# Sliding-window attention and a spectral mix on one core: more weight buffers at the end of the attention stage, a new order of stage memory, and x moved within the forward transform

## The chip, the core and the metric

The kernel runs on one core of a Trainium2 chip. Its engines are called here as the profile calls them: PE (TensorE, matmuls; PEld are its weight loads), DVE (VectorE), ACT (ScalarE), POOL (GpSimd) and SP (SyncE). Data come from HBM over 16 DMA engines into SBUF, the memory of 128 partitions that all engines read; matmuls write to PSUM. The metric is the device time of one execution in microseconds, the median of several runs.

## What is computed

Two parts follow each other. The first is attention with a causal window of 64 positions, for 8 batches of 8 heads, 576 positions of 64 numbers. The second takes the attention's output as x (8 x 576 x 512), transforms it along the sequence, multiplies each of the lowest 64 modes by its own complex 512 x 512 matrix, transforms back, adds x, and passes the sum through one more 512 x 512 matrix.

```python
# attention, per batch and head
scores = q @ k.T / sqrt(64)
mask = (rel >= 0) & (rel < 64)           # rel = query position - key position
x = softmax(where(mask, scores, -1e9)) @ v
# spectral mix, x now [8, 576, 512]
X = rfft(x, axis=1)
Xr, Xi = X[:, :64].real, X[:, :64].imag
Yr = einsum('bmd,mde->bme', Xr, w_r) - einsum('bmd,mde->bme', Xi, w_i)
Yi = einsum('bmd,mde->bme', Xr, w_i) + einsum('bmd,mde->bme', Xi, w_r)
u = x + irfft(Yr + 1j * Yi, n=576)
out = u + maximum(u @ w_ch, 0)
```

All inputs are fp32 in HBM. The two sets of mode weights, w_r and w_i, are 64 matrices of 1 MB each, 134 MB in all. They are read once, and cast to bf16 by the DMA on the way: each of the 128 weights is 512 KB in SBUF, 4,096 bytes in every partition.

## The kernel before

The kernel has three stages, and the weights are loaded beneath the first two.

**The attention stage** goes over 36 windows of 8 blocks of 64 queries. For each batch it loads q, k and v, transposes q and k and regroups v with matmuls (ten "units" a batch, spread over the windows), adds the mask by a matmul with an identity, adds the scores, takes the exponential on ACT, and weighs v with it. The sums land in `pso` and DVE divides them into `x_sb`. When a batch is complete, `dft` makes its forward transform into `XQ`. Every load is issued by POOL, in program order.

```python
VW = 4 * 17; LW = 5; EW = 13
x_sb = keep.tile([128, B, NT, NC, 128], BF16, name="x_sb")

def load_w(i, pool, tag, wt=None):
    m, im = divmod(i, 2)
    if wt is None:
        wt = pool.tile([128, NC, DM], BF16, name="wt", tag=tag)
    src = moe_w_i if im else moe_w_r
    nc.gpsimd.dma_start(out=wt, in_=src[m].rearrange("(p c) e -> p c e", c=NC))
    wtiles[i] = wt

def mask(w, times):
    for _ in range(times):
        for hh in range(2):
            nc.tensor.matmul(out=pss[(2 * w + hh) % 3], lhsT=ident_bf,
                             rhs=view(band, 0, [[0, WIN // 128], [1, 128]]), ...)
# ... in weigh(), when a head is complete:
rcp = small.tile([128, 2, NT * 4], FP32, name="rcp")
nc.vector.reciprocal(out=rcp, in_=view(pso, 16, [[512, 2], [17, NT * 4]]))
nc.vector.tensor_tensor(
    out=view(x_sb, b * NT * DM + g * 16, [[64, 2], [128, NT * 4], [1, 16]]),
    in0=view(pso, 0, ...), in1=view(rcp, 0, ...), op=ALU.mult)

def dft(b):
    ps = ps_misc.tile([128, NC, 2, NM], FP32, name="psx", tag="misc")
    for c in range(NC):
        for t in range(NT):
            n = rows(t)
            nc.tensor.matmul(out=ps[:, c, :, :], lhsT=x_sb[:n, b, t, c, :],
                             rhs=trigF[:n, t, :], start=(t == 0), stop=(t == NT - 1))
    nc.vector.tensor_copy(out=view(XQ, ...), in_=ps...)
    nc.scalar.mul(out=view(XQ, ...), in_=ps[:, :, 1, :], mul=-1.0)
```

The heads' columns stand in `x_sb` in an order that suits the transform's weight loads, (part of a head, head, 16 columns), and not in the order of the output.

The weights' buffers in this stage: 5 in `wlate` and 13 in `wearly`, loaded two at the start and three behind each batch's units; then the buffers of q, k and v of the last two batches as those become free (`spare_raw`, three for each); then, at window 32, batch 6's kT and the two halves of its vt.

```python
def unit(b, j):
    units[b][j]()
    if j == NU - 1:                     # the last of ten units of a batch
        if b + 2 < B:
            load(b + 2)                 # q, k, v two batches ahead
        early(3)                        # weights into wlate, wearly
        if b >= B - 2:
            early(EARLY)
            spare_raw()
# ... at the end of window w:
if w == -(-9 * (B - 1) // 2):
    i = (B - 2) % 2
    spare(kTs[i])
    for j in range(2):
        spare(vts[i][:, j])
```

**The mode stage** multiplies mode by mode: 32 matmuls a mode, 16 columns each. It starts with eight more weight buffers, `wmid`, and then goes round the five `wlate` buffers. Beside the first 48 modes it transposes x and multiplies it by w_ch (`channel`, 36 tiles). For that, each tile of `x_sb` is first put into the order of the output, by a copy on ACT and one back on DVE. Beside the last 16 modes it turns the lower part of the spectrum back and adds it to the channel product (`spectrum`, `second`).

```python
late = p2.enter_context(tc.tile_pool(name="late", bufs=1, side="right", ...))
YT, YTl = ...; trigI, trigL = ...; wch = late.tile([128, NC, DM], FP32R, name="wch")
Z0a = late.tile([128, 33, DM], FP32R, name="Z0a")
MW = 8
wmid = wm.enter_context(tc.tile_pool(name="wmid", bufs=MW, side="right", ...))
while nw < MID:                          # MID = nw + MW
    load_w(nw, wmid, "wm"); nw += 1
# ... after each mode m:
while nw < 2 * NM and (nw - MID if nw < MID + LW else nw - LW) <= 2 * m + 1:
    load_w(nw, wlate, "wl"); nw += 1

def channel(i):
    ...
    xc = xtp.tile([128, NC, 128], BF16, name="xc")
    nc.scalar.copy(out=xc[:n], in_=x_sb[:n, bb, tt, :, :])                      # L493
    nc.vector.tensor_copy(out=view(x_sb[:n], (bb * NT + tt) * DM, [[NC, 128], [1, NC]]),
                          in_=view(xc[:n], 0, [[1, 128], [128, NC]]))           # L494
    ...  # transpose, copy, four matmuls by wch, copy to Z0
```

The scheduler puts these two copies early: they run in the attention stage.

**The output stage** begins when mode 63 is done: `turn` brings back the last 16 modes, `group` sums four tiles at a time, and SP writes them out. All its matmuls on `Yb`, `trigI`, `trigL`, `Z0` are of 512 columns.

Of the kernel before, what the change touches and what calls it, by code (L numbers as in the profile page):

```python
# [26 lines left out]
def kernel(  # L27
# [19 lines left out]
    VW = 4 * 17  # L47
    RUN = S // 32
    LW = 5
    EW = 13  # L50

# [20 lines left out]
    x_sb = keep.tile([128, B, NT, NC, 128], BF16, name="x_sb")  # L72
# [10 lines left out]
    etp = p1.enter_context(tc.tile_pool(name="etp", bufs=4, side="right"))  # L83
    small = p1.enter_context(tc.tile_pool(name="small", bufs=2, side="right"))
# [51 lines left out]
    def gen_trig(pool, mt, n, dst_cos, dst_sin, tag):  # L136

        f = pool.tile([128, 2, n], FP32, name="gf" + tag)
        r = pool.tile([128, 2, n], FP32, name="gr" + tag)
# [8 lines left out]
    with tc.tile_pool(name="tmpf", bufs=1, side="right") as tmp:  # L148
        mo = tmp.tile([128, NM], FP32, name="mo")
        to = tmp.tile([128, NT], FP32, name="to")  # L150
        mt = tmp.tile([128, NT * NM], FP32, name="mtf")
# [4 lines left out]
        nc.vector.tensor_tensor(out=view(mt, 0, [[NM, NT], [1, NM]]), in0=view(mo, 0, [[0, NT], [1, NM]]),  # L156
                                in1=view(to, 0, [[1, NT], [0, NM]]), op=ALU.mult)
        gen_trig(tmp, mt, NT * NM, trigF[:, :, 0:NM], trigF[:, :, NM:2 * NM], "f")
# [15 lines left out]
    band = acons.tile([128, 128], BF16, name="band")  # L174
    nc.vector.memset(band, 0.0)
    for half in range(2):
        pp = slice(64 * half, 64 * half + 64)
        own = band[pp, 64 * half:64 * half + 64]
        nxt_ = band[pp, 64 - 64 * half:128 - 64 * half]
# [9 lines left out]
    vts = [p.tile([128, 2, 4, 9, 4, 17], BF16, name=f"vt{i}") for i, p in enumerate((aeven, acons))]  # L189
    for vt in vts:  # L190
        nc.vector.memset(vt[:, 0, :, :, :, 16:17], 1.0)
# [12 lines left out]
    def transpose_units(b):  # L204
# [18 lines left out]
        def vpart(a, j0, j1):  # L223
            def f():
# [8 lines left out]
                for i in range(2):  # L233
                    evac(vt[:, 0, 2 * a + i, j0:j1, :, 0:16],
                         view(pss[i], 0, [[D, n], [1, 4], [4, 16]]), i == 0)
# [14 lines left out]

    def mask(w, times):

        for _ in range(times):
            for hh in range(2):
                nc.tensor.matmul(out=pss[(2 * w + hh) % 3], lhsT=ident_bf,  # L255
                                 rhs=view(band, 0, [[0, WIN // 128], [1, 128]]),
                                 start=True, stop=False, skip_group_check=True)
# [28 lines left out]
    def weigh(w, G0, G1):  # L286
        et = ets[w]
        for hh in range(2):
            for G in range(G0, G1):
# [7 lines left out]
                nc.tensor.matmul(out=pso[po, hh, (i // 2) * VW:(i // 2 + 1) * VW],  # L297
                                 lhsT=et[pk, hh, col:col + 64],
                                 rhs=vt[pk, 1 - f % 2, 2 * hh + g // 2, f // 2, :, :],
                                 start=True, stop=True, skip_group_check=True)  # L300
        if G1 > G0 and G1 % 9 == 0:

            rcp = small.tile([128, 2, NT * 4], FP32, name="rcp")
            nc.vector.reciprocal(out=rcp, in_=view(pso, 16, [[512, 2], [17, NT * 4]]))
            nc.vector.tensor_tensor(  # L305
                out=view(x_sb, b * NT * DM + g * 16, [[64, 2], [128, NT * 4], [1, 16]]),
                in0=view(pso, 0, [[512, 2], [17, NT * 4], [1, 16]]),
                in1=view(rcp, 0, [[NT * 4, 2], [1, NT * 4], [0, 16]]), op=ALU.mult)
            if g == 3:
                dfts.append(b)  # L310

    def dft(b):
        ps = ps_misc.tile([128, NC, 2, NM], FP32, name="psx", tag="misc")
        for c in range(NC):
            for t in range(NT):
                n = rows(t)
                nc.tensor.matmul(out=ps[:, c, :, :], lhsT=x_sb[:n, b, t, c, :],  # L317
                                 rhs=trigF[:n, t, :], start=(t == 0), stop=(t == NT - 1))
# [5 lines left out]
    EARLY = LW + EW  # L324

    def early(n):
        nonlocal nw
        for _ in range(n):
            if nw < EARLY:
                load_w(nw, wlate if nw < LW else wearly, "wl" if nw < LW else "we")  # L330
# [422 lines left out]
```

The softmax here doesn't subtract the row's maximum and nothing guards it: scores larger than these inputs give would overflow.

## Time and profile before

| | |
|---|---|
| time, median of 3 runs | 450.59 us (449.89 to 457.41) |
| span of the profiled execution | 449.9 us |
| PE busy | 343.5 us (76%) |
| DVE busy | 209.4 us (47%) |
| ACT busy | 156.1 us (35%) |
| POOL busy | 131.5 us (29%) |
| moved by DMA | 92.49 MB, 206 GB/s in the mean |
| read from HBM, written to it | 163.58 MB, 9.44 MB |

How to read it: busy shares are averages over three stages that have different limits, so a stage has to be looked at by itself. The strip of 40 slices shows how full each engine is as time goes on, 11.25 us to a slice; PEclk in it is the matmul clock that was granted, in tenths; GB/s counts the bytes as they are written, and a weight is written at half the size at which it is read. The attention stage ends at about 148 us, the last weight lands at 405.4 us, and what follows is the output stage. A group's line gives how many instructions, their busy time and the mean of one, and then how long the engine was idle before them and for what.

### The profile page before, as it was taken

How to read it: one execution, taken by the hardware profiler on the slowest of the kernel's cores; microseconds unless marked ns; L12 is line 12 of the kernel's file. 1: busy time of each engine (PE TensorE's matmuls, PEld its weight loads, DVE VectorE, ACT ScalarE, POOL GpSimd, SP SyncE). 2: the span in 40 equal slices, each digit the busy share in tenths (PEclk: the TensorE clock that was granted, in tenths of full speed). 3: DMA queues.
4: the chain of work that ended last, by engine and by line, in shares of the span. 5: the costliest groups of instructions: out<-in, count | busy, mean ns of one | idle time of the engine just before them, and what ended most of it. 6: DMA issues, size and time to landing. Idle time of an engine off the chain costs nothing.

```text
span 449.9 us, 11402 instructions
## 1 busy us (share of the span) xinstructions
PE 343.5 (76%) x4996; PEld 223.8 (50%) x4996; DVE 209.4 (47%) x412; ACT 156.1 (35%) x295; POOL 131.5 (29%) x218
## 2 busy tenths in 40 slices
PE   6899999999999765588887874322275775898994
PEld 2366556556655665465565653212253443555552
DVE  4466897888876400145545421000024433344774
ACT  4566776767865300041233221000010100103563
POOL 8632532442120411122222221121122122112574
PEclk9989999999999555595889998555555657698999
DMA  8999999999997799999999999999999999990787
GB/s 139 206 209 208 212 210 208 212 208 208 214 169 146 136 213 213 258 205 213 203 214 213 214 212 215 214 212 214 213 214 213 213 210 212 215 194 23 245 298 276
DMA packets 38338, 92.49 MB, mean 206 GB/s; under 512 B 3472, under 2 KB 12688, under 8 KB 38288
## 3 DMA queue, kind: packets, MB, share of 16 engines
q0 software_dynamic: 33040, 82.32, 94.9%
q1 hardware_dynamic: 5248, 9.44, 5.9%
q8 instruction: 39, 0.64, 0.5%
q14 instruction: 11, 0.09, 0.1%
HBM read 163.58 MB, written 9.44 MB: 385 GB/s over the span
## 4 chain that ended last, share of the span: by engine, by line
DMA 37%; PE 26%; issue 17%; DVE 8%; POOL 5%; ACT 5%; POOLq 1%; ACTq 0%; DVEq 0%
DMA wt<-in_moe_w_r_dram 26%; DMA wt<-in_moe_w_i_dram 9%; PE pso L297 4%; DVE x_sb L494 3%; POOL wt L119 3%; PE psx L317 3%; PE psc L680 2%; PE psu L698 2%; DMA rv<-in_v_dram 2%; PE pst L216 2%; PE pss_186 L255 2%; ACT et L279 1%; PE pss_184 L255 1%; ACT xc L493 1%; PE pss_185 L255 1%
## 5 line engine op out<-in xcount | busy, mean ns | idle before, releaser
L465 PE MATMUL psy<-XQ,wt 128*128 128x16 bf16 x960 | 58.8, 191 | 51.3 <-DMA wt<-in_moe_w_i_dram 51.1
L119 POOL DMA_DIRECT2D wt<-in_moe_w_i_dram x60 | 33.2, 553 | 180.3 <-PE psy L465 147.1
L460 PE MATMUL psy<-XQ,wt 128*128 128x16 bf16 x944 | 60.6, 191 | 32.0 <-DMA wt<-in_moe_w_r_dram 25.4
L465 PEld LDWEIGHTS <-wt 128*128 128x128 bf16 x960 | 45.7, 104 | 63.0 <-DMA wt<-in_moe_w_i_dram 61.6
L460 PEld LDWEIGHTS <-wt 128*128 128x128 bf16 x944 | 45.6, 104 | 47.7 <-DMA wt<-in_moe_w_r_dram 37.0
L503 PE MATMUL psz<-wch,xT 128*128 128x512 f32 x144 | 49.9, 481 | 1.7 <-DMA wch<-in_moe_w_ch_dram 1.7
L500 DVE CAST xT<-pxt 128x512 fp32r<-128x512 bf16 x36 | 24.2, 687 | 53.3 <-PE pxt L497 37.5
L505 ACT CAST Z0a<-psz 128x512 fp32r<-128x512 f32 x33 | 19.4, 586 | 66.4 <-PE psz L503 51.9
L59 DVE CAST YT<-psy 128x256 fp32r<-128x256 f32 x6 | 2.5, 424 | 75.8 <-PE psy L465 75.8
L119 POOL DMA_DIRECT2D wt<-in_moe_w_r_dram x59 | 32.0, 543 | 17.0 <-PE psy L465 6.2
L620 DVE TENSOR_TENSOR Z0a<-pse,Z0a 128x512 fp32r<-128x512 f32 x33 | 21.8, 688 | 31.5 <-PE pse L597 31.5
L503 PEld LDWEIGHTS psz<-wch,xT 128*128 128x128 f32 x144 | 30.1, 230 | 6.9 <-DMA wch<-in_moe_w_ch_dram 1.8
L708 POOL TENSOR_TENSOR ot<-ot,r 128x512 f32<-128x512 f32 x18 | 22.8, 1283 | 24.7 <-ACT Yb L58 19.5
L297 PEld LDWEIGHTS <-et 128*64 128x64 bf16 (+1 forms) x576 | 22.3, 108 | 15.0 <-issue 8.0
L493 ACT COPY xc<-x_sb 128x512 bf16<-128x512 bf16 (+1 forms) x40 | 23.9, 619 | 15.1 <-DVE x_sb L494 8.8
L58 ACT CAST YT<-psy 128x256 fp32r<-128x256 f32 x6 | 2.2, 373 | 71.7 <-DVE YT L59 59.0
L494 DVE COPY x_sb<-xc 128x512 bf16<-128x512 bf16 (+1 forms) x40 | 23.1, 598 | 8.2 <-PE psx L317 3.8
L305 DVE TENSOR_TENSOR x_sb<-pso,rcp 128x640 bf16<-128x640 f32 x32 | 26.4, 824 | 1.1
L103 POOL DMA_DIRECT2D rv<-in_v_dram x32 | 20.7, 653 | 9.7 <-PE psv_348 L231 3.6
L701 ACT ACTIVATE r<-psc 128x512 f32<-128x512 f32 x36 | 19.0, 601 | 10.2 <-PE psc L686 9.6
L597 PE MATMUL pse<-yw,trigI 96*128 96x512 f32 x40 | 20.6, 584 | 0.0
L614 ACT CAST yw<-psw 96x512 fp32r<-96x512 f32 x8 | 4.7, 583 | 44.8 <-PE psw L610 44.8
(298 smaller groups left out, 668.1 us busy)
## 6 DMA issues: line engine op xcount, KB each, us to landing
wt<-in_moe_w_i_dram POOLq DMA_DIRECT2D x60, 512.0 KB, 8.6
wt<-in_moe_w_r_dram POOLq DMA_DIRECT2D x59, 512.0 KB, 10.6
out_dram<-ot SPq DMA_DIRECT2D x32, 256.0 KB, 2.4
rk<-in_k_dram POOLq DMA_DIRECT2D x8, 576.0 KB, 11.1
rq<-in_q_dram POOLq DMA_DIRECT2D x8, 576.0 KB, 10.5
rv<-in_v_dram POOLq DMA_DIRECT2D x32, 144.0 KB, 10.0
wch<-in_moe_w_ch_dram POOLq DMA_DIRECT2D x1, 1024.0 KB, 15.7
out_dram<-ot SPq DMA_DIRECT2D x8, 128.0 KB, 2.5
```

Source lines behind the costliest of these rows:

```text
L103: nc.gpsimd.dma_start(out=rv[32 * hp:32 * hp + 32, :, :, :].rearrange("r j c d -> r j (c d)"), in_=vf[hp].rearrange("(j r c) d -> r j (c d ...
L119: nc.gpsimd.dma_start(out=wt, in_=src[m].rearrange("(p c) e -> p c e", c=NC))
L297: nc.tensor.matmul(out=pso[po, hh, (i // 2) * VW:(i // 2 + 1) * VW], lhsT=et[pk, hh, col:col + 64], rhs=vt[pk, 1 - f % 2, 2 * hh + g // 2, ...
L305: nc.vector.tensor_tensor(out=view(x_sb, b * NT * DM + g * 16, [[64, 2], [128, NT * 4], [1, 16]]), in0=view(pso, 0, [[512, 2], [17, NT * 4 ...
L460: nc.tensor.matmul(out=psy[:, m % MG, e, :], lhsT=wr[:, c, ee], rhs=XQ[:, c, :, 1:3, m], start=(c == 0), stop=False)
L465: nc.tensor.matmul(out=psy[:, m % MG, e, :], lhsT=wi[:, c, ee], rhs=XQ[:, c, :, 0:2, m], start=False, stop=(c == NC - 1))
L493: nc.scalar.copy(out=xc[:n], in_=x_sb[:n, bb, tt, :, :])
L494: nc.vector.tensor_copy(out=view(x_sb[:n], (bb * NT + tt) * DM, [[NC, 128], [1, NC]]), in_=view(xc[:n], 0, [[1, 128], [128, NC]]))
L500: nc.vector.tensor_copy(out=xT, in_=pst)
L503: nc.tensor.matmul(out=psz, lhsT=xT[:, c, :], rhs=wch[:, c, :], start=(c == 0), stop=(c == NC - 1))
L620: nc.vector.tensor_tensor(out=channel_out(i), in0=ps, in1=channel_out(i), op=ALU.add)
L708: nc.gpsimd.tensor_tensor(out=ot, in0=ot, in1=r, op=ALU.add)
```

## The change

The change works on four things.

- **Room for weights in the attention stage.** One more early buffer (`wextra`), and more of the last two batches' own buffers: at window 32 batch 6's kT and vt as before and a qT, at windows 35 and 36 batch 7's kT, a qT and its vt. The early loads are spread thinner, two behind a batch instead of three.
- **Stage memory.** `late` holds only YT, YTl and wch. The seven `wmid` buffers come right behind it, so that they lie on the early buffers 6 to 12, and each is loaded as soon as the mode that used that buffer is done (`free_at`). The tables and Z0 (now one tile) come last, over the attention's memory. `Yb` and `yw` use the wmid buffers afterwards.
- **x in the forward transform.** DVE writes `x_sb` in the order of the output right away, so that the two copies of L493 and L494 are gone. The transform takes the table as its stationary side and 512 columns of x at once, five matmuls in place of 20; the result is copied by ACT and turned by four transposes one window later (`dft_turn`).
- **Smaller things.** From window 6 the mask is added in four 64 x 64 pieces; batch 1's units have another order; the tables are made in smaller pieces; four idle matmuls follow mode 63; there are 11 output buffers instead of 9.

```diff
-    VW = 4 * 17
+    VW = 66
+    XW = 1
-    x_sb = keep.tile([128, B, NT, NC, 128], BF16, name="x_sb")
+    x_sb = keep.tile([128, B, NT, DM], BF16, name="x_sb")
@@ band: two halves -> two patterns for each half of the partitions
-    band = acons.tile([128, 128], BF16, name="band")
-    for half in range(2):
+    band = acons.tile([128, 2, 128], BF16, name="band")
+    for i in range(4):                    # two affine_selects each
@@ mask
+                if w < 6:
+                    ...                   # as before, from band2
+                    continue
+                for half in range(2):
+                    pp = slice(64 * hh, 64 * hh + 64)
+                    nc.tensor.matmul(out=pss[(2 * w + hh) % 3][64 * half:64 * half + 64, :],
+                                     lhsT=ident_bf[pp, pp],
+                                     rhs=view(band[pp], 128 * half, [[0, WIN // 128], [1, 128]]),
+                                     start=True, stop=False, skip_group_check=True)
@@ weigh
-            rcp = small.tile([128, 2, NT * 4], FP32, name="rcp")
+            rcp = small.tile([128, 2, NT], FP32, name="rcp")
-                out=view(x_sb, b * NT * DM + g * 16, [[64, 2], [128, NT * 4], [1, 16]]),
+                out=view(x_sb, b * NT * DM + g * D, [[4 * D, 2], [DM, NT], [1, D]]),
@@ dft
-        for c in range(NC):
-            for t in range(NT):
-                nc.tensor.matmul(out=ps[:, c, :, :], lhsT=x_sb[:n, b, t, c, :],
-                                 rhs=trigF[:n, t, :], start=(t == 0), stop=(t == NT - 1))
+        for t in range(NT):
+            n = rows(t)
+            nc.tensor.matmul(out=ps, lhsT=trigF[:n, t, :], rhs=x_sb[:n, b, t, :],
+                             start=(t == 0), stop=(t == NT - 1))
+        Xs[b] = xsp.tile([128, NC, 128], BF16, name="Xs")
+        evac(Xs[b], view(ps, 0, [[1, NC], [NC, 128]]), True)
+    def dft_turn(b):
+        ps = ps_misc.tile([128, NC, 2, NM], BF16, name="pxq", tag="misc")
+        for c in range(NC):
+            nc.tensor.transpose(out=ps[:, c, :, :]..., in_=Xs[b][:, c, :], identity=ident_bf)
@@ early weights
-    EARLY = LW + EW
+    EARLY = LW + EW + XW
-        early(2)                          # at the start
+        early(1)
+            order = (1, 2, 4, 5, 7, 8, 0, 3, 6, 9) if b == 1 else range(NU)
-                early(3)                  # behind a batch
+                early(2)
@@ spares
-            if w == -(-9 * (B - 1) // 2):
-                i = (B - 2) % 2
+            if w in (NWIN - 4, NWIN - 1):
+                i = (B - 2) % 2 if w == NWIN - 4 else (B - 1) % 2
                 spare(kTs[i])
+                spare(qtp.tile([128, 4, S], BF16, name="qT"))
+            if w in (NWIN - 4, NWIN):
+                i = (B - 2) % 2 if w == NWIN - 4 else (B - 1) % 2
                 for j in range(2):
                     spare(vts[i][:, j])
@@ memory and weights of the mode stage
-    trigI = late.tile(...); trigL = late.tile(...); Z0a = late.tile([128, ZA, DM], ...)
+    MW = 7
+    wmid = p2.enter_context(tc.tile_pool(name="wmid", bufs=MW, side="right", ...))
+    late2 = ...                           # trigI, trigL, Z0
-    while nw < MID:
-        load_w(nw, wmid, "wm")
+    N0 = nw
+    free_at = [(LW + 6 + j) // 2 for j in range(MW)]
+        while nw < 2 * NM:                # after each mode m
+            j = nw - N0
+            if j < LW:
+                at, pool, tag = j // 2, wlate, "wl"
+            elif j < LW + MW:
+                at, pool, tag = free_at[j - LW], wmid, "wm"
+            elif j < 2 * LW + MW:
+                at, pool, tag = (nw - LW - MW) // 2, wlate, "wl"
+            else:
+                at, pool, tag = (nw - LW) // 2, wlate, "wl"
+            if m < at:
+                break
+            load_w(nw, pool, tag)
@@ channel
-                nc.scalar.copy(out=xc[:n], in_=x_sb[:n, bb, tt, :, :])
-                nc.vector.tensor_copy(out=view(x_sb[:n], ...), in_=view(xc[:n], ...))
-        Z_M = 15
+        Z_M = 17
@@ end
+                    idle(4)               # behind mode 63
-        op = p3.enter_context(tc.tile_pool(name="op", bufs=9, ...))
+        op = p3.enter_context(tc.tile_pool(name="op", bufs=11, ...))
```

## The prediction, made before the change was run

> **What bounds the kernel now.** I read four views, in this order: the page's strip of 40 slices with the queue and chain parts, to find the resource that stays full; the busy time by stretches around the one place where it isn't; the GpSimd engine's order of time there, to see who holds the transfers back; and the chain of waits through two batches of the attention stage, to see what that stage is made of.
>
> From the page (a slice is 11.25 us):
>
> ```profile
> PE   6899999999999765588887874322275775898994
> PEclk9989999999999555595889998555555657698999
> DMA  8999999999997799999999999999999999990787
> GB/s 139 206 209 208 212 210 208 212 208 208 214 169 146 136 213 213 258 205 213 203 214 213 214 212 215 214 212 214 213 214 213 213 210 212 215 194 23 245 298 276
> q0 software_dynamic: 33040, 82.32, 94.9%
> DMA 37%; PE 26%; issue 17%; DVE 8%; POOL 5%; ACT 5%; POOLq 1%; ACTq 0%; DVEq 0%
> ```
>
> The transfers are the only thing full from start to 405 us. The matmul clock sits at half speed over much of the mode stage, which is itself a sign of a PE that waits. Three weak spots: the first slice, slices 12 to 14 (169, 146 and 136 GB/s), and the output stage after the last weight. The 82.32 MB of queue 0 at the 213 GB/s of the full slices is 386 us; the loads end at 405.4. So about 19 us less some start-up is what a perfect schedule could still win.
>
> By stretches of 5 us (engine, busy us and count; then clock, DMA share, GB/s):
>
> ```profile
> 120.00:125.00 5.00, 4.80 (x84) 2.74 (x82) 4.81 (x10) 4.66 (x10) 0.53 (x1) 1.00 1.06 204
> 125.00:130.00 5.00, 4.65 (x81) 2.71 (x79) 4.56 (x9) 3.56 (x8) 1.06 (x2) 1.00 0.88 155
> 130.00:135.00 5.00, 4.75 (x77) 2.55 (x78) 2.79 (x6) 2.17 (x4) 1.42 (x3) 1.00 1.03 179
> 135.00:140.00 5.00, 5.00 (x66) 2.88 (x64) 2.85 (x6) 3.00 (x6) 0.16 (x1) 1.00 1.06 213
> 140.00:145.00 5.00, 4.36 (x82) 2.68 (x81) 3.32 (x7) 2.90 (x6) 0.00 (x0) 1.00 0.57 116
> 145.00:150.00 5.00, 3.83 (x45) 2.56 (x44) 2.79 (x5) 1.14 (x2) 1.55 (x3) 0.77 0.08 7
> 150.00:155.00 5.00, 4.05 (x104) 3.57 (x104) 3.97 (x7) 2.75 (x5) 3.43 (x7) 0.50 1.01 193
> ```
>
> Against 213 the shortfalls are 9 + 58 + 34 + 0 + 97 + 206 + 20 = 424 GB/s, times 5 us = 2.12 MB, which is **9.95 us of transfer** at 213.
>
> GpSimd, which issues every load, in order of time there:
>
> ```profile
> 134.10 0.53 POOL L119 DMA_DIRECT2D vt_178<-in_moe_w_r_dram  x1 [2.56 <-PE pso L297]
> 134.62 0.54 POOL L119 DMA_DIRECT2D vt_178<-in_moe_w_i_dram  x1
> 148.45 0.53 POOL L119 DMA_DIRECT2D wt<-in_moe_w_i_dram  x1 [13.29 <-DVE x_sb L305]
> ```
>
> After the ninth spare buffer there is nowhere to put weight 27: the next place lies over attention memory and waits 13.29 us for the last x write. That is the hole.
>
> The chain of waits from 73 to 105.1 us, two batches, by line:
>
> ```profile
> by line: PE pso L297 12.8%; DVE x_sb L494 12.0%; PE psx L317 10.7%; PE pst L216 6.0%; PE pss_186 L255 5.2%; ACT xc L493 5.2%; ACT et L279 4.9%; PE pss_184 L255 4.7%; DVE XQ L320 3.7%; PE pss_185 L255 3.4%; DVE qT L59 2.7%; DVE x_sb L305 2.6
> ```
>
> No DMA is in it: the attention stage runs at the pace of its engines. One batch takes 16.05 us (the transforms' first matmuls stand at 40.86, 72.96 and 105.06 us). Its transfers are rk 576 + rq 576 + rv 4 x 144 KB and three weights of 512 KB, 3,264 KB = 3.34 MB, or 16.0 us at 209 GB/s. So compute and transfers are matched there, and that must be watched when either changes.
>
> **What the Trainium skill says.** *Perfetto Trace Analysis*, section "Roofline": one core alone is bounded by its 16 DMA engines at about 435 GB/s. The queue writes bf16 and reads fp32, so 213.5 GB/s written is 427 read: the trace agrees, and no change of buffers will make a full slice fuller. *DMA: Bandwidth & Descriptors*, "Anatomy of one DMA — SWDGE (gpsimd) path": DMA engines don't wait on semaphores; the issuing sequencer does, before dispatch. The 13.29 us above, with 7 GB/s at the end of it, is that. *TensorEngine Tiling (Array Packing)*, "Key Properties": tiles of the array work independently, and a change of tiling mode drains it. The trace agrees on the first: 18 score matmuls on 64x64 tiles, of 64 to 128 columns, pass in 0.35 us (85.97 to 86.32 in the chain), where one 512-column mask takes 0.22. It shows no drain by itself. *TensorE: Matmul & The Clock Gate*, "Part 1: The HAM clock gate": an idle window of some 3.4 us halves the clock; the 0.50 from 150 to 180 us, with PE waiting for weights, agrees.
>
> **The change, part by part.**
>
> *More room for weights.* Before, 18 early buffers, 6 raw buffers and 3 of batch 6 make 27 weights in the attention stage. After: 19 early, 6 raw, 4 at window 32 (kT, qT, two halves of vt), 2 at window 35, 2 at 36: 33. Transfers up to there: 14.16 MB of q, k, v plus 33 x 0.524 = 31.5 MB, at 209 to 213 about 149 us, so the queue has work until about 152 us even if nothing else follows. The hole began because 28.3 MB were done at about 137.
>
> *Recycling at once.* YT, YTl and wch now take 24.6 KB a partition, just six weight buffers, and the seven wmid buffers lie on the early buffers 6 to 12, freed by modes 5 to 8. With five wlate buffers (modes 0 to 2) and wch, 14 units of 2.46 us = 34 us of transfers come free once mode 8 is done. A mode whose weights are there costs little: 126 matmuls in 155 to 160 us are four modes in 5 us at half clock. Nine modes are some 11 us, beside the leftover of the spares. The next release is mode 16; its weights land before the 34 us are used up. I count no new hole. Gain of these two parts: up to **9.95 us**.
>
> *x in the forward transform.* The 40 copies of L493 (23.9 us of ACT) and 40 of L494 (23.1 us of DVE) go. On the chain they are 12.0 + 5.2 = 17.2% of 32.1 us, 2.8 us a batch. The transform goes from 20 matmuls (about 2.0 us a batch) to 5 of 512 columns at 0.22 plus 4 transposes at about 0.1: 0.5 us less, with one more evacuation on ACT of about 0.6, not on PE's path since the transposes stand a window later. The masks become four 64x64 pieces from window 6: 13 a batch at 0.22 = 2.9 us; if the pieces overlap as the scores do, up to 1.4 us less; if not, nothing or a little more. Sum: 16.05 - 2.8 - 0.5 - (0 to 1.4) = 11.4 to 12.8 us of compute a batch. Transfers a batch fall to 2,752 KB (two weights instead of three), 13.5 us. So a batch should take about **13.5 us and become bound by transfers**; attention ends near 130 us instead of 148. That shortens nothing by itself: the weights not loaded early must still be loaded. It is worth something only because the queue stays full.
>
> *Small things.* Eight band selects instead of four at the start: 4 x about 0.19 us ahead of the second load, **+0.7**. Batches that don't quite reach 13.5 us: **+0.5**. Four idle matmuls after mode 63, which may keep the clock up for the first turn (its four matmuls took 1.83 us against 1.00 for the second turn), and 11 output buffers, though no wait for an output buffer stands in the list: **-0.5**. The 44.5 us after the last load otherwise stay.
>
> Sum: 450.6 - 9.95 + 0.7 + 0.5 - 0.5 = 441.3; I say **441.0**.
>
> **Rivals.** (1) *The attention stage doesn't get shorter*: mask pieces run one after another, or another engine binds. With 16 us a batch and 13.5 us of transfers, 2.5 us are lost in each of about five batches, 12.5 us in place of the 9.95 saved: 453. With 14.5 us a batch, 5 us are lost: 446. Against it: 17% of the chain is plainly taken out; for it: PE is busy 31.1 of 32.1 us, though with the tails of pipelined matmuls counted. (2) *The hole moves*: nothing is released between modes 8 and 16, and 5-deep recycling follows. If mode 16 is late the queue runs dry for some us: 443 to 446. (3) *All of the shortfall goes*, start included: the loads end near 391, and with 44.5 us behind them the time is 436. That is a floor as long as the output stage is untouched. (4) *The output stage changes by itself* through the clock: its first 3 us windows granted 0.85 and 0.58; worth 1 us either way.
>
> **Range and chances.** The floor gives the low end, 436; the half-failed attention stage gives the high end, 447. 2% is 441.6, right beside my value: faster by over 2% 0.53, within 2% 0.42, slower by over 2% 0.05, the last for rival 1 in full and worse.
>
> **What would show it.** Right: transfers at 205 GB/s or more in every slice from the second to the one where loads end; that end at 394 to 397; no GpSimd wait of over 5 us on an x write; the transforms 13 to 14 us apart; the last x write near 130 us; the output stage 44 to 45 us. Wrong: slices of 180 GB/s within the attention stage (rival 1), a dip 15 to 40 us after it (rival 2), or an output stage that is longer or shorter by 2 us, which none of my terms has.

## The result, and the profile after

| | before | after |
|---|---|---|
| time, median of 4 runs | 451.29 us (449.89 to 457.41) | 444.56 us (442.79 to 445.58) |
| ratio to before, 95% interval | | 0.9857 [0.9808, 0.9906] |
| span of the profiled execution | 449.9 us | 441.0 us |
| last weight landed | 405.4 us | 397.7 us |
| last x written | 147.8 us | 144.1 us |
| from the last weight to the end | 44.5 us | 43.3 us |

The kernel became 1.4% faster, 6.7 us by the medians. Predicted were 441.0 us and 9.6 us. The profiled execution is the fastest of the four, so its 8.9 us flatter the change a little: 7.7 us of them are the earlier end of the loads and 1.2 us a shorter output stage, which changes from one execution to the next (e12). A second set of runs on another chip is among the experiments (e5).

The strip of 40 slices of the changed kernel, with its queue and its chain (a slice is 11.0 us):

```profile
PE   6999999948998665122268886988576685899994
PEclk9999999986998555555558899686765856699998
DMA  8999999999999999999999999999999999991787
GB/s 138 196 207 209 213 209 208 212 209 213 209 213 214 214 214 232 238 214 209 197 213 202 213 202 211 212 214 214 213 213 214 215 213 213 213 189 40 246 301 273
q0 software_dynamic: 33040, 82.32, 96.7%
DMA 46%; PE 28%; issue 18%; POOL 3%; ACT 3%; DVE 1%; POOLq 0%; ACTq 0%
```

The dent of slices 12 to 14 is gone. Two things are new: PE has a hole of its own in the ninth slice, followed by a lower clock, and the transfers have more small dents than before, in slices 19, 20, 22 and 24 (209, 197, 202, 202).

The same stretches as were shown of before (engine, busy us and count; then clock, DMA share, GB/s):

```profile
120.00:125.00 5.00, 4.42 (x89) 2.78 (x88) 2.70 (x6) 3.74 (x8) 0.53 (x1) 1.00 1.06 211
125.00:130.00 5.00, 5.00 (x118) 3.31 (x115) 3.77 (x8) 2.80 (x6) 1.14 (x3) 1.00 1.06 212
130.00:135.00 5.00, 4.65 (x97) 2.70 (x96) 2.09 (x5) 2.24 (x5) 2.04 (x4) 1.00 1.07 215
135.00:140.00 5.00, 4.43 (x70) 2.29 (x73) 2.28 (x5) 2.71 (x6) 0.00 (x0) 1.00 1.06 213
140.00:145.00 5.00, 3.22 (x60) 2.44 (x62) 2.09 (x4) 1.08 (x2) 2.12 (x4) 0.60 1.06 213
145.00:150.00 5.00, 3.39 (x47) 1.88 (x47) 0.42 (x1) 0.97 (x2) 0.00 (x0) 0.50 1.07 215
150.00:155.00 5.00, 3.70 (x126) 3.62 (x123) 0.00 (x0) 0.00 (x0) 3.19 (x6) 0.50 1.06 212
```

Not one of them is under 211 GB/s. The hole of 9.95 us is closed in full. POOL's order of time shows how: the spare buffers come one after another, and the first ordinary buffer follows with a wait of 5.72 us instead of 13.29, for which the queue has work enough.

```profile
133.03 0.54 POOL L121 DMA_DIRECT2D vt_204<-in_moe_w_i_dram  x1
140.80 0.53 POOL L121 DMA_DIRECT2D kT_203<-in_moe_w_i_dram  x1 [7.22 <-PE pso L318]
141.38 0.53 POOL L121 DMA_DIRECT2D qT<-in_moe_w_r_dram  x1
143.32 0.53 POOL L121 DMA_DIRECT2D vt_205<-in_moe_w_i_dram  x1 [1.41 <-PE pso L318]
143.84 0.54 POOL L121 DMA_DIRECT2D vt_205<-in_moe_w_r_dram  x1
150.10 0.53 POOL L121 DMA_DIRECT2D wt<-in_moe_w_i_dram  x1 [5.72 <-PE psy L505]
```

The chain from 73 to 105.1 us, the stretch that held no transfer before:

```profile
by line: DMA rv<-in_v_dram 53.5%; DMA wt<-in_moe_w_i_dram 42.3%; PE pst L223 4.4%; PE psv_2253 L238 3.5%; PE pso L318 2.7%; PE pss_210 L275 1.8%; PE pss_210 L294 1.2%; issue 1.0%; PE psv_2252 L238 0.3%; PE pss_211 L294 0.1%; PE pss_211 L275
```

In this stretch the attention stage is now bound by transfers, above all by one load of v. The reason is in POOL's order of time again:

```profile
72.10 0.53 POOL L121 DMA_DIRECT2D wt<-in_moe_w_r_dram  x1 [1.96 <-DMA wt<-in_moe_w_i_dram]
75.43 0.53 POOL L121 DMA_DIRECT2D wt<-in_moe_w_i_dram  x1 [2.80 <-DMA rq<-in_q_dram]
76.45 0.73 POOL L97 DMA_DIRECT2D rk<-in_k_dram  x1 [0.49 <-PE psv_1791 L238]
77.17 0.58 POOL L121 DMA_DIRECT2D wt<-in_moe_w_r_dram  x1
78.03 0.71 POOL L97 DMA_DIRECT2D rq<-in_q_dram  x1 [0.28 <-issue]
78.73 0.56 POOL L121 DMA_DIRECT2D wt<-in_moe_w_i_dram  x1
81.36 0.66 POOL L105 DMA_DIRECT2D rv<-in_v_dram  x1 [2.07 <-PE psx L340]
```

In the program two weights stand behind each batch's q, k and v. Here weights stand before and between them: the scheduler, which turns the program into the order of each engine's instructions, has put weights ahead of a v that waits for a buffer. By 106 us, when the last v is issued, 17 weights are out; the order of the program would have had 9. PE pays for it with 6.7 us of waiting (PE psv_2252 for rv), its clock is at half from 96.7 to 106.9 us, and the stage ends at 144 us instead of the 130 that I had worked out.

The kernel before isn't in program order throughout either, contrary to what I said of it. From batch 6 on weights stand between k and q there too:

```profile
77.23 0.73 POOL L95 DMA_DIRECT2D rk<-in_k_dram  x1 [5.52 <-PE pst L216]
77.95 0.97 POOL L119 DMA_DIRECT2D wt<-in_moe_w_i_dram  x1
81.28 0.71 POOL L95 DMA_DIRECT2D rq<-in_q_dram  x1 [2.37 <-PE pst L216]
```

But it has only 16 weights ahead of its last v (102.87 us) where its program has 14.

To see where the rest of the expected gain went, I took from one trace of each kernel the shortfall of the transfers against 213 GB/s, stretch by stretch, in us: the sum of (213 - GB/s) x length / 213 over stretches of 10 and 20 us until the last weight lands. w_ch, which is not cast, is written at twice the rate of a weight and lies between 160 and 200 us, so 2.46 us are added there.

| kernel | 0-20 | 20-120 | 120-160 | 160-200 | 200-300 | 300-end | sum | last weight |
|---|---|---|---|---|---|---|---|---|
| before | 4.3 | 1.6 | **10.0** | 0.4 | 0.5 | 1.5 | 18.3 | 405.4 |
| after | 4.7 | 1.6 | **0.0** | 0.0 | **2.3** | 1.9 | 10.4 | 397.7 |
| after, once more (e5) | 4.9 | 1.5 | 0.0 | 0.0 | **3.6** | 2.5 | 12.4 | 400.0 |
| old x path (e1) | 4.8 | 1.6 | 0.3 | 0.0 | 3.7 | 1.8 | 12.2 | 399.6 |
| new x path alone (e8) | 4.3 | 1.6 | 9.3 | -0.1 | -0.2 | 3.0 | 17.8 | 404.9 |
| fewer spares (e3) | 4.8 | 1.7 | 8.4 | 0.0 | 0.8 | 1.2 | 16.9 | 404.1 |
| program order (e4) | 4.9 | 2.3 | -0.1 | 0.0 | 1.8 | 1.2 | 10.1 | 397.2 |
| ring of 12 (e6) | 4.9 | 1.7 | 5.5 | -0.1 | -0.2 | 2.6 | 14.4 | 401.8 |
| combined (e7) | 4.2 | 4.6 | 0.0 | -0.1 | -0.3 | 4.9 | 13.3 | 400.8 |
| order + ring (e9) | 5.0 | 6.1 | 0.0 | -0.1 | -0.4 | 4.5 | 15.1 | 402.6 |
| order + ring + split (e10) | 4.3 | 3.9 | -0.1 | -0.1 | -0.2 | 3.4 | 11.2 | 398.7 |
| order + whole masks (e11) | 5.0 | 4.4 | -0.1 | 0.0 | 1.9 | 2.9 | 14.1 | 401.2 |
| no idle matmuls (e12) | 5.0 | 3.2 | -0.1 | 0.0 | 1.2 | 1.7 | 11.0 | 398.3 |

In every row the last weight lands at 387.1 to 387.6 us plus the sum. That is bookkeeping and no finding: every kernel moves the same bytes, so what is not moved at 213 GB/s must appear as shortfall. What the table tells is where each kernel loses it. Behind the last weight each kernel has an output stage of 43.3 to 44.6 us, so the end of the loads sets the time to within 1.3 us. The two profiles of the changed kernel show the bargain: 10.0 us are won in the hole, and 1.8 to 3.1 are given back between 200 and 300 us, 0.4 to 1.0 in the last stretch and 0.4 to 0.6 at the start.

### The profile page after: what moved, and what is told of

It reads as the page before. It is cut to its first block, busy times and chain, and to the rows that moved or that the text cites. A ratio compares the mean times of both kernels' runs of the same rounds, so it can differ in the third digit from the quotient of the medians.

```text
span 441.0 us, 11418 instructions
## 1 busy us (share of the span) xinstructions
PE 328.7 (75%) x4989; PEld 218.9 (50%) x5002; DVE 187.8 (43%) x393; ACT 141.4 (32%) x269; POOL 129.2 (29%) x217
## 3 DMA queue, kind: packets, MB, share of 16 engines
q0 software_dynamic: 33040, 82.32, 96.7%
## 4 chain that ended last, share of the span: by engine, by line
DMA 46%; PE 28%; issue 18%; POOL 3%; ACT 3%; DVE 1%; POOLq 0%; ACTq 0%
DMA wt<-in_moe_w_r_dram 31%; DMA wt<-in_moe_w_i_dram 11%; DMA rv<-in_v_dram 4%; PE pso L318 3%; POOL wt L121 3%; PE psc L727 2%; PE pss_212 L378 2%; PE pst L223 2%; PE psu L745 2%; PE psx L340 2%; PE psy L505 1%; PE psy L500 1%; PE psc L733 1%; PE psu L740 1%; ACT et L300 1%
## 5 line engine op out<-in xcount | busy, mean ns | idle before, releaser
L505 PE MATMUL psy<-XQ,wt 128*128 128x16 bf16 x912 | 56.2, 191 | 47.1 <-DMA wt<-in_moe_w_i_dram 47.0
L500 PE MATMUL psy<-XQ,wt 128*128 128x16 bf16 x912 | 58.1, 191 | 34.6 <-DMA wt<-in_moe_w_r_dram 29.8
L121 POOL DMA_DIRECT2D wt<-in_moe_w_i_dram x57 | 30.7, 538 | 178.1 <-PE psy L505 154.6
L505 PEld LDWEIGHTS <-wt 128*128 128x128 bf16 x912 | 43.8, 104 | 58.4 <-DMA wt<-in_moe_w_i_dram 56.9
L500 PEld LDWEIGHTS <-wt 128*128 128x128 bf16 x912 | 44.3, 104 | 45.7 <-DMA wt<-in_moe_w_r_dram 36.3
L546 PE MATMUL psz<-wch,xT 128*128 128x512 f32 x144 | 47.7, 477 | 1.0 <-DVE xT L543 1.0
L548 ACT CAST Z_3232<-psz 128x512 fp32r<-128x512 f32 x36 | 21.1, 587 | 76.0 <-PE psz L546 76.0
L121 POOL DMA_DIRECT2D wt<-in_moe_w_r_dram x57 | 30.9, 541 | 37.7 <-PE psy L505 13.9
L666 DVE TENSOR_TENSOR Z_3232<-pse,Z_3232 128x512 fp32r<-128x512 f32 x36 | 23.7, 688 | 34.0 <-PE pse L644 33.4
L755 POOL TENSOR_TENSOR ot<-ot,r 128x512 f32<-128x512 f32 x18 | 22.8, 1286 | 23.2 <-ACT Yb_5588 L59 13.3
L238 PEld LDWEIGHTS <-pick 32*128 32x128 bf16 x256 | 10.8, 93 | 15.4 <-DMA rv<-in_v_dram 6.8
L318 PE MATMUL pso<-vt_204,et 128*64 128x65 bf16 (+1 forms) x288 | 17.1, 204 | 0.0
L300 ACT ACTIVATE et<-pss_211 128x512 bf16<-128x512 f32 x24 | 14.3, 597 | 7.4 <-PE pss_212 L294 7.4
L318 PE MATMUL pso<-vt_205,et 128*64 128x65 bf16 (+1 forms) x288 | 16.1, 208 | 0.5 <-DVE x_sb L326 0.5
## 6 DMA issues: line engine op xcount, KB each, us to landing
rq<-in_q_dram POOLq DMA_DIRECT2D x8, 576.0 KB, 13.3
qT<-in_moe_w_r_dram POOLq DMA_DIRECT2D x2, 512.0 KB, 12.4
```

Source lines behind the costliest of these rows:

```text
L318: nc.tensor.matmul(out=pso[po, hh, (i // 2) * VW:(i // 2) * VW + D + 1], lhsT=et[pk, hh, col:col + 64], rhs=vt[pk, 1 - f % 2, 2 * hh + g / ...
L500: nc.tensor.matmul(out=psy[:, m % MG, e, :], lhsT=wr[:, c, ee], rhs=XQ[:, c, :, 1:3, m], start=(c == 0), stop=False)
L505: nc.tensor.matmul(out=psy[:, m % MG, e, :], lhsT=wi[:, c, ee], rhs=XQ[:, c, :, 0:2, m], start=False, stop=(c == NC - 1))
L546: nc.tensor.matmul(out=psz, lhsT=xT[:, c, :], rhs=wch[:, c, :], start=(c == 0), stop=(c == NC - 1))
L548: nc.scalar.copy(out=channel_out(i), in_=psz)
L666: nc.vector.tensor_tensor(out=channel_out(i), in0=ps, in1=channel_out(i), op=ALU.add)
```

## The experiments

Each is the changed kernel with one edit, unless it says otherwise; ratios are to the kernel before on the same chip. A few executions of a kernel come out slower as a whole: medians and ranges include them, ratios leave them out.

**e1: the old x path with the new buffers.**

```diff
-    dft: 5 matmuls of 512 columns, Xs, dft_turn; pieces of masks
+    dft: 20 matmuls of 128 columns; whole masks
+    for t in range(NT):                      # right behind each dft
+        xc = xsp.tile([128, NC, 128], BF16, name="xc")
+        nc.scalar.copy(out=xc[:n], in_=x_sb[:n, b, t, :, :])
+        nc.vector.tensor_copy(out=view(x_sb[:n], ...), in_=view(xc[:n], ...))
```

> The changed kernel with the old x path put back: 20 matmuls a transform, the two copies of every x tile (placed in the attention stage right behind the transform), whole masks; all the buffers and the memory order of the change stay. Theory A (the gain is the closed hole in the loads and nothing else; weights go ahead of q, k, v in the queue whenever engines are slow): 444 to 446 us, loads at 205 GB/s or more through 150 us. Theory B (the shorter engine work of the attention stage is needed, because two weights a batch leave the queue idle for 2.5 us of each 16 us batch): 449 us or more, slices of 180 GB/s between 40 and 100 us.

Measured: 445.93 us, ratio 0.9857 [0.9760, 0.9953], the same ratio as the whole change. The hole is 0.3 us, and the shortfall from 20 to 120 us is 1.6 as before and after the change. Theory A holds: the longer engine work costs nothing that this interval lets one see; 16 weights are issued ahead of the last v, so the queue has work while the engines are slow. The new x path is not where the time comes from.

**e2 and e8: the new x path alone,** in the kernel before, with its buffers, masks and early loads. The tables are made in pieces, as in the change.

```diff
 (the kernel before)
-    x_sb = keep.tile([128, B, NT, NC, 128], BF16, name="x_sb")
+    x_sb = keep.tile([128, B, NT, DM], BF16, name="x_sb")
+    dft, dft_turn, rcp and vt as in the change; no copies L493, L494
+    tables made in pieces
```

> The kernel before with only the new x path (five matmuls and four transposes a transform, no copies of x tiles; the tables made in pieces so that it fits), with its own buffers and its own mask. Theory A: the hole lasts from about 139 us until the attention stage ends; that end moves only by what the engines gain after the last q, k, v has landed (about 105 us), some 4 us, so 446 to 448 us, with a hole of 5 to 7 us left. Theory B (a batch falls to 13.5 us throughout): attention ends near 130 us, no hole, 441 to 443 us.

Measured: 450.32 us, ratio 0.9972 [0.9945, 0.9999]. Theory B is out; theory A had the direction right and too large a size. The profile that is read here is that of e8, the same kernel:

> The kernel before with only the new x path, once more, for a profile in which the attention stage is undisturbed. From its 20 times of before (median 450.3): the queue runs dry near 139 us and the last x is written at 144 to 146 us, 2 to 4 us sooner than in the kernel before; where the other 2 to 3 us went must be seen.

Measured, one execution: 450.01 us. The last x is written at 144.7 us, 3.1 us sooner than before. But POOL's first ordinary buffer comes at 147.69 us against 148.45, and the hole shrinks from 10.0 to only 9.3 us:

```profile
132.68 0.54 POOL L120 DMA_DIRECT2D vt<-in_moe_w_i_dram  x1
147.69 0.53 POOL L120 DMA_DIRECT2D wt<-in_moe_w_i_dram  x1 [14.48 <-ACT Xs L58]
```

The wait is now put down to ACT's Xs, the copy that the new transform has and the old one had not. It is done at 146.71 us, and the transposes that read it at 147.16: the memory of the next buffers is held by the last transform instead of the last x. Of the 3.1 us that the engines gain, 0.8 reach the loads. This is where the other 2 to 3 us went.

**e3: fewer spare buffers.**

```diff
-            if w in (NWIN - 4, NWIN - 1):    # kT and qT
-            if w in (NWIN - 4, NWIN):        # both halves of vt
+            if w == NWIN - 4:                # kT and both halves of vt of batch 6
```

> The changed kernel with the spare buffers of the last two batches cut back to those of the kernel before (kT and the two halves of vt at window 32; no qT, nothing at windows 35 and 36): 28 weights in the attention stage instead of 33. Theory A: the queue is dry from about 140 us to about 151 us, 11 us are lost again: 454 to 457 us. Rival (the hole would have closed anyway because early buffers are recycled at once): 445 to 447 us.

Measured: 450.44 us, ratio 0.9984 [0.9960, 1.0009]: nearly the kernel before again. The hole is back, at the same place in POOL's order:

```profile
133.39 0.54 POOL L121 DMA_DIRECT2D vt<-in_moe_w_r_dram  x1
150.13 0.53 POOL L121 DMA_DIRECT2D wt<-in_moe_w_r_dram  x1 [16.21 <-PE psy L502]
```

What ends the wait is not the same: the next buffer is a `wlate` one here, and it comes free with the first mode's matmuls (PE psy), not with the last x. In both kernels POOL waits for the attention stage to end because no buffer is left. The mechanism is as theory A has it, and without the five spare buffers the whole gain is gone; the rival is out, and the new order of memory alone brings nothing. Whether the spare buffers would close the hole in the old order of memory was not tested. The size was too large: the hole is 8.4 us and not 11, and the stretch from 200 to 300 us loses 0.8 us instead of the 2.3 to 3.6 of the changed kernel.

**e4: the loads of the attention stage in the order of the program.**

```diff
-    with tc.manual_schedule(engines={mybir.EngineType.PE}):
+    with tc.manual_schedule(engines={mybir.EngineType.PE, mybir.EngineType.Pool}):
```

> The changed kernel with the loads of the attention stage issued in the order of the program: two weights behind each batch's q, k, v, none ahead of them. Theory A (the attention stage lost 9 us around 91 to 100 us because eight weights went ahead of v, but transfers bind everywhere): attention ends 10 us or more earlier, near 135 us, and the time stays at 443 to 446 us. Rival C (an earlier end of the attention stage is worth time, since the mode stage gets slack): 439 to 442 us. Rival D (the queue now has gaps in each batch): 447 us or more, slices of 190 GB/s between 40 and 100 us.

Measured: 444.22 us, ratio 0.9819 [0.9744, 0.9893]. The last x is written at 133.0 us, 11 us sooner, with the clock at full speed until then, and the last weight lands only 0.5 us sooner (397.2 against 397.7). Rival D is out, and so is rival C by the end of the loads, though not by the interval of the times; the queue loses 2.3 us instead of 1.6 from 20 to 120 us. But theory A's "transfers bind everywhere" fails within the stage. The chain from 73 to 105.1 us:

```profile
by line: PE pso L318 21.7%; PE psv L238 18.8%; PE pss L275 14.8%; PE pst L223 13.4%; PE pss L294 8.5%; PE psx L340 7.7%; ACT qT L59 5.0%; ACT et L300 5.0%; ACT kT L59 4.4%; issue 1.2%; ACTq L300 0.0%
```

No DMA is in it. In program order the attention stage runs at the pace of its engines, as in the kernel before, and a batch takes 14.4 us (the transforms of every second batch start at 38.09, 66.97 and 95.86 us). That the stage of the changed kernel waits for transfers comes from the order of its loads.

**e5: the changed kernel once more,** beside e6 and e7.

> The changed kernel once more, beside the next two on one chip. Same ratio as before, 0.982 to 0.989, 443 to 446 us.

Measured: 445.56 us (443.63 to 446.58), ratio 0.9870 [0.9832, 0.9907].

**e6: a ring of 12 weight buffers** until mode 46.

```diff
-            elif j < 2 * LW + MW:
-                at, pool, tag = (nw - LW - MW) // 2, wlate, "wl"
+            elif j < 5 * (LW + MW):
+                at = (nw - LW - MW) // 2
+                pool, tag = (wlate, "wl") if j % (LW + MW) < LW else (wmid, "wm")
+            elif j < 5 * (LW + MW) + LW:
+                at, pool, tag = (nw - LW - MW) // 2, wlate, "wl"
```

> The changed kernel with the seven wmid buffers used for weights again and again until mode 46, so that 12 buffers go round instead of 5 between modes 16 and 46. Theory A2 (what the change gives back, some 2 us of transfers between 200 and 280 us, is the ring of five: a load waits for a mode that waits for channel matmuls at half clock): GB/s of 212 or more from 200 to 280 us, loads end 1.5 to 2.5 us earlier, 442 to 443 us. Rival (the DMA itself is slower there, from the reads and writes of the table and channel work in SBUF): the dips stay, time within 0.5 us of the changed kernel.

Measured: 443.38 us (442.33 to 447.24), ratio 0.9842 [0.9793, 0.9891]. The channel stretch of the changed kernel (the first three lines are of its trace; the last three columns are clock, DMA share and GB/s):

```profile
210.00:220.00 10.00, 2.54 (x64) 2.12 (x64) 6.79 (x21) 1.24 (x5) 2.23 (x5) 0.50 1.04 195
230.00:240.00 10.00, 8.68 (x136) 7.33 (x134) 4.29 (x7) 2.75 (x5) 2.58 (x5) 1.00 1.04 200
260.00:270.00 10.00, 8.75 (x135) 6.99 (x134) 3.87 (x6) 3.08 (x6) 2.23 (x5) 1.00 1.04 204
```

and the same stretches with the ring of 12:

```profile
210.00:220.00 10.00, 2.60 (x64) 2.17 (x64) 7.96 (x30) 1.61 (x6) 2.11 (x4) 0.50 1.07 214
230.00:240.00 10.00, 9.65 (x100) 7.88 (x101) 2.58 (x4) 2.34 (x4) 2.12 (x4) 0.72 1.06 213
260.00:270.00 10.00, 8.52 (x124) 6.74 (x122) 3.64 (x6) 3.19 (x6) 2.11 (x4) 1.00 1.07 214
```

With the same table and channel work beside them the transfers are full, so the rival is out: a deeper ring takes the dents away, and 2.3 to 3.6 us go to -0.2 (-0.2 to -0.4 in e7, e9 and e10, which have the ring as well). The reason that theory A2 gives for them, modes that wait for channel matmuls at half clock, isn't shown: the dent from 210 to 220 us lies ahead of the first channel matmul (226.0 us), with PE busy for 2.54 of 10 us. And a part of the gain is lost again: behind 300 us the four kernels with the ring lose 2.6 to 4.9 us, the changed kernel 1.9 and 2.5. From 200 us to the end of the loads that is 2.4 to 4.6 us with the ring, 4.2 and 6.1 in the changed kernel, but 3.0 and 2.9 in e4 and e12, which have the ring of five, so a gain over the whole is not shown.

The profiled execution took 446.88 us, one of two near 447 among six, because the hole came back in it:

```profile
115.00:125.00 10.00, 10.00 (x165) 6.69 (x165) 5.91 (x11) 4.85 (x10) 1.06 (x2) 0.50 1.12 214
125.00:130.00 5.00, 4.78 (x80) 2.67 (x79) 1.80 (x5) 3.04 (x6) 0.53 (x1) 0.86 0.74 148
130.00:135.00 5.00, 4.42 (x89) 2.75 (x89) 3.48 (x7) 3.65 (x8) 0.53 (x1) 1.00 0.67 108
135.00:140.00 5.00, 4.65 (x102) 2.71 (x98) 3.19 (x8) 2.70 (x6) 2.25 (x5) 1.00 0.96 149
```

In the changed kernel's trace the clock was back at full speed at 106.9 us; here it stays at half from 95.7 to 126.4. The engines give batch 7's raw buffers free at 129.2 us instead of 122.4, and the queue is dry: 5.5 us. The ring isn't in use yet at that time, so this is a difference between executions and not the edit.

**e7: program order, ring of 12, three early weights behind batch 3, and the second batch's load ahead of the band selects.**

```diff
+    load(1)                                  # ahead of the eight selects
     NEG = -30000.0
-                early(2)
+                early(3 if b == 3 else 2)
     (and the edits of e4 and e6)
```

> The changed kernel with the ring of 12, the loads of the attention stage in program order (three weights instead of two behind batch 3, where the queue had run dry), and the second batch's load issued ahead of the eight band selects. Theory A2: the gains add, 2 us from the ring and 0.6 us from the start; loads end near 394.5 us, 440.5 to 442.5 us. Rival (once the queue is full, something else sets the pace and the end stays): within 0.5 us of the changed kernel.

Measured: 445.78 us, ratio 0.9877 [0.9853, 0.9902]. The gains did not add. The start is better (4.2 against 4.9) and the channel stretch full, but from 20 to 120 us 4.6 us are lost. In its list of waits:

```profile
PE pss L269 <- DVE band L261: 2.3, 1, 2.3
```

and two stretches of 2 us:

```profile
46.00:48.00 2.00, 1.55 (x15) 0.62 (x13) 1.19 (x3) 1.63 (x5) 0.00 (x0) 1.00 0.77 93
50.00:52.00 2.00, 2.00 (x54) 1.31 (x53) 1.85 (x5) 1.66 (x5) 1.39 (x3) 1.00 0.59 53
```

The selects, moved behind the load, hold up the first mask by 2.3 us. That the queue is dry 25 us later because of it is not shown: e9, which leaves the selects in place, is dry in the same stretches (90 and 105 GB/s). The last stretch also loses 4.9 us, 2.6 of it from 320 to 360 us, where the ring goes back to five.

**e9 and e10: program order and ring alone; then q and k of the second batch ahead of the selects and its v behind them.**

```diff
     (e9: the edits of e4 and e6)
+    load_qk(1)                               # e10 only
     NEG = -30000.0
     ...
-    load(1)
+    load_v(1)                                # e10 only
```

> The changed kernel with the loads of the attention stage in program order and the ring of 12, and nothing else. Theory A3 (what the weights that go ahead of v cost is a matmul clock at half speed from about 95 us on, which in some executions lasts until 126 us and then leaves the queue dry for 5 us; in program order it can't happen): times with less scatter, 440.5 to 442.5 us, 210 GB/s or more from 200 to 280 us, full clock until attention ends near 133 us. Rival (the scatter of 442 to 447 us is of the DMA and has nothing to do with the order): median and scatter as in the run with the ring alone, 443 to 444 us.

Measured: 445.64 us (442.74 to 447.71), ratio 0.9882 [0.9833, 0.9932]. Full transfers from 200 to 300 us as expected, but theory A3 falls: the scatter is no smaller. In the profiled execution the clock was at half from 28.6 to 38.8 us, in the attention stage's first windows; POOL then waited 10.30 us for the next rk buffer at 45.85 us, and 6.1 us are lost from 20 to 120 us. So program order doesn't keep a slow clock from leaving the queue dry. Nor is a slow clock needed: e10 loses 3.9 us in the same stretch with its clock at full speed from 9.9 to 132.7 us.

> As the one before, with the second batch's q and k issued ahead of the eight band selects and its v behind them. Theory: the start gains back the 0.6 us of the selects without making the first mask wait as in the combined version: 0.3 to 0.8 us less than the one before. Rival (selects 1.5 us later again hold up the first mask and with it the early batches): 1 us or more above it, queue dry between 44 and 52 us.

Measured: 445.33 us (441.70 to 455.08), ratio 0.9848 [0.9788, 0.9908]. The start is 4.3 instead of 5.0, so the 0.6 us of the selects come back, and no wait for the mask appears. From 48 to 50 us the queue is dry all the same (129 GB/s). Whether the time follows can't be told from intervals this wide.

**e11: whole masks in program order.**

```diff
-                if w < 6:
+                if w < NWIN:                 # and the edit of e4
```

> The changed kernel with loads in program order and whole 128 x 128 masks in every window; to be read against the run in program order with mask pieces, whose last x is written at 133 us. If the pieces overlap four at a time they save 1.4 us a batch: last x 6 to 9 us later, 139 to 142 us. If they don't overlap: 133 us. The time hardly moves either way, 443 to 446 us, since the loads bind.

Measured, one execution: 446.3 us. DVE's writes of x from 90 to 140 us in e4 (first line) and here, with the first and the last start in us:

```profile
L326 DVE TENSOR_TENSOR x_sb<-pso,rcp x14: 814/824/825, 90.7 to 132.2; 128x640 bf16<-128x640 f32 x14
```

```profile
L326 DVE TENSOR_TENSOR x_sb<-pso,rcp x15: 815/824/825, 91.1 to 139.3; 128x640 bf16<-128x640 f32 x15
```

The stage ends 7.1 us later, with the clock at full speed until then in both. Pieces are used from window 6 to 35, 6.7 batches, so by this one pair of executions they save 1.06 us a batch, or 0.15 us for each of 46 pairs of masks; a pair took 0.44 us whole. They overlap, though not fourfold throughout. The slower stage also leaves the queue dry for 4.4 us in place of 2.3, so in program order the engines' pace may count for the time; one execution doesn't show it.

**e12: without the idle matmuls behind mode 63.**

```diff
-                    idle(4)
+                    pass
```

> The changed kernel without the four idle matmuls behind mode 63. My term for them was -0.5 us. If they keep the clock up, the first turn's four matmuls take 1.6 us or more in place of 1.0 and the time is 0.5 to 1 us longer than the changed kernel's, 445 to 446.5 us; if not, no difference that the scatter of 2 us lets one see.

Measured: 445.96 us, ratio 0.9882 [0.9853, 0.9910], not to be told from the changed kernel's 0.9870. In this profile the first turn's four matmuls (psl, then pslw) take 1.85 us, as before the change (1.83), and the output stage 44.6 us. But e5, with the idle matmuls, has 1.63 us and 44.6, and e8, without them, 1.0 us and 43.3. In e5 the idle matmuls (psd) stand on the chain themselves; its chain first, then that of e12:

```profile
401.03 1.65 PE psd L676 x4
402.67 0.47 PE psl L712 x4
403.14 1.63 PE pslw L714 x4
```

```profile
400.29 0.56 PE psl L712 x4
400.85 1.85 PE pslw L714 x4
```

At half clock they take 1.65 us, and the turn starts 2.67 us after the last weight landed instead of 1.96: what they bring back sooner, they have cost. In the five profiles whose clock is at half for 3.4 us behind the last weight (before, e1, e5, e7, e12) the output stage takes 44.2 to 44.6 us, in the eight others 43.3 or 43.4. Three of the five have the idle matmuls, so they don't decide it.

**No version here is clearly faster than the changed kernel.** The ring of 12 has the lowest median beside it on one chip, 443.38 against 445.56, and their intervals overlap.

## Why the prediction was right or wrong

*The hole, -9.95 us:* right. It went from 10.0 to 0.0, and e3 shows that the spare buffers did it.

*34 us of loads free after mode 8, no gap until mode 16:* right, though 13 loads stand there and not 14, or 32 us: w_ch isn't cast and reads as many bytes as a weight, so it counts once. From 160 to 200 us the shortfall is 0.0.

*x in the forward transform:* right in its value, wrong in its course. I said that it shortens nothing by itself; e1 is as fast without it, and alone (e2) it brings 0.3%. But "attention ends near 130 us" failed: 144 us. The step took the order of the program for the order of the loads. In program order (e4) the stage ends at 133 us, and there the other half of the step fails: a batch takes 14.4 us, not 13.5, and is bound by its engines, not by transfers, so the 11.4 to 12.8 us of compute were too few. The masks' "0 to 1.4 us" measured 1.06 a batch; which other term was short isn't known. None of this cost time, since weights filled the queue: where rival 1 counts 5 us for 14.5 us a batch, e4 loses 0.7 more than before.

*Recycling, "I count no new hole":* this is the step that failed. The term of the sum that it left out, 0 in the prediction, measured +1.8 to +3.1 us between 200 and 300 us, and e6 takes it away there by a deeper ring alone. Rival 2 named such a loss, with times of 443 to 446 us, and put it in the wrong place. The prediction has no term for the ring of five, which kept the queue full in the kernel before (213 GB/s). The kernel before does its channel products from 187 to 275 us, the changed kernel from 226 to 312. Why five buffers lost only 0.5 us there before, nothing in e8, and 0.8 and 1.2 in e3 and e12, which have the memory order of the change, isn't settled by these runs.

*Small things:* the start, +0.7, measured 0.4 to 0.6, and e10 gets it back. The +0.5 for batches that fall short measured 0.0 (1.6 us from 20 to 120 us, as before). The -0.5 of the output stage is not the idle matmuls (e12); the stage takes some 43.3 or 44.5 us by the clock that the first turn happens to get. The last stretch, for which I had no term, lost 0.4 to 1.0 us more.

The columns of the table, after less before, give -10.0 + 0.4 - 0.4 + 1.8 + 0.4 = -7.8 us for the last weight, against 405.4 - 397.7 = 7.7 measured; with e5's profile -10.0 + 0.6 - 0.1 - 0.4 + 3.1 + 1.0 = -5.8 against 5.4. The 6.7 us of the medians lie between. So the time fell inside the range, and most of what is missing from the 9.6 us is the loss that the sum didn't have.

*Signs:* of those that the prediction named, the end of the loads (397.7 us against 394 to 397), the last x and the output stage (43.3 against 44 to 45) missed, and four slices were under 205 GB/s (196, 197, 202, 202). No x write held POOL.

*What was taken from the Trainium skill:* the bound by 16 DMA engines and the wait in the issuing sequencer carried the argument. No slice of the changed kernel in which only cast weights move is above 215 GB/s, and in e3 and e8 the hole lies at the end of POOL's waits of 16.21 and 14.48 us. That a changed tiling mode drains the array was not tested by itself.

## What to carry to other kernels

When one resource is full nearly throughout, add up its shortfall stage by stage against the rate of its full stretches. The sum itself only restates when the transfers end, but its columns show which stage loses the time, and a change is worth what it takes out of them and not what it takes off an engine. When one hole is closed, ask of each ring of buffers behind it how much is in flight: five buffers lost up to 3.7 us here where twelve lost none, and twelve lost more behind them. And look in the trace at the order in which loads are issued before reckoning with it: a scheduler may move loads that wait for nothing ahead of the ones that the engines need next.

## What the runs showed that I had not expected

The half clock can outlast the wait that it comes with: with one wait of 6.7 us for v it stayed for 10 us in the changed kernel (96.7 to 106.9) and for 31 us in e6 (95.7 to 126.4), though by the profile PE was busy for 10.0 of the 10 us from 115 to 125. It also came without any such wait, from 28.6 to 38.8 us in e9 and to 38.9 in e12. Behind it the queue went dry for 5.5 us in e6, and in e9 the stretch from 20 to 120 us lost 3.8 us more than in e4, which has the same order of loads and kept the full clock. That is as much as most of the edits here.
